# Small VectorE instructions of the tile tables and of the weight scales read one operand from PSUM

## Chip, core and metric

The kernel runs on one core of one Trainium2 chip. The metric is device time in microseconds (us) for one execution, in runs of the same program. Names of engines in the profile: PE is TensorE (PEld its weight loads), DVE is VectorE, ACT is ScalarE, POOL is GpSimd, SP is the queue that issues most DMAs.

## What is computed

Two layers in sequence: a causal convolution whose seven weights per head and position come from a softmax, then a mixture of experts that sends each of 28,672 tokens to one of eight experts.

```python
def _attn_ref(x, weight_gen):              # x (8, 3584, 192), weight_gen (8, 3584, 8, 7)
    w = np.exp(weight_gen - np.max(weight_gen, axis=-1, keepdims=True))
    w = w / (np.sum(w, axis=-1, keepdims=True) + 1e-09)
    x_pad = np.concatenate([np.zeros((B, pad, D)), x], axis=1)
    x_unf = x_pad[:, idx, :].reshape(B, S, K, H, group)
    return np.einsum('bshk,bskhg->bshg', w, x_unf).reshape(B, S, D)

def _moe_ref(x, w_gate, w_output_gate, w1, w2):   # x (28672, 192), w1 (8, 192, 1024), w2 (8, 1024, 192)
    logits = x @ w_gate
    e_idx = np.argmax(logits, axis=1)
    gate_w = probs[np.arange(N), e_idx]           # probs: softmax of logits
    eom = 1.0 / (1.0 + np.exp(-(x @ w_output_gate)))
    for e in range(E):
        mask = e_idx == e
        ye = np.maximum(x[mask] @ w1[e], 0.0) @ w2[e]
        out[mask] = gate_w[mask, None] * eom[mask, e, None] * ye
```

## The kernel before

**Units.** The tokens pass in 32 units of 896 (128 partitions by 7 rows). For each unit the seven weights per head go through a softmax (`softmax_steps`, line 506), seven products of shifted inputs with a weight are formed and added up (`tap_steps`, `acc_steps`). GpSimd forms five of the seven products in the later units (`gap` in the profile), VectorE the other two (into `ps` and `vt`), and VectorE adds all of them into an accumulator in PSUM; in the first seven units TensorE does the adding (`vap` and `gap` with `cf`). The sum is scaled and split into two float16 parts (`rt`), the expert is found (`sum_steps`), the position of each token in its expert's list is worked out (`place_steps`), and GpSimd scatters the rows into a sorted buffer in DRAM (`srtd`, seven indirect DMAs per unit).

**Tables of tiles.** After each unit a round decides how many tiles of T sorted tokens (512 in most rounds, 128, 256 or 384 in a few) have become full. `round_table` (line 844) works it out for R tiles at most on one partition of VectorE: `f_nE` is the number of tokens that each expert has and that no tile has taken (from `bs` and `done`); `gg` compares it with what the r-th tile needs; `cs` is a running count over experts; `f_cx` is that count, clipped to R, at each expert's end; `zt` is the row where an expert's next tile would begin, less T times the tiles counted before it; `ge` compares the count with r; `done` moves on; `dz` is the difference of neighbouring `zt`; two sums over `ge` then give the expert and the first row of each tile (`ti`), which SP reads into registers to load the tile. Small values that VectorE uses lie in `few`, columns 2320 to 2512 of the one PSUM tile `ps`, under names that begin with `f_`.

**Weights.** Eight experts' weights are loaded in float32, scaled by powers of two and split into two float16 parts (`split_steps`, line 431), in the first stage of the kernel. `scales` (line 375) takes the exponent of a sum of squares (`ex`) and makes of it the scale and its inverse; it works on two columns for weights (`wss` to `wsc` and `winv`), on one column for units (`ssq` to `sx` and `isx`) and for the gate.

**Tiles.** For each tile SP loads the sorted rows transposed (`xT`) and the expert's weights (`wa`, `wb`). TensorE makes the first product (`ps<-xT,wa`), ScalarE applies Relu into the float16 part `hh`, VectorE takes the rest of the value into `hl`, and TensorE makes the second product from `hh` and `hl`. ScalarE scales the result (`ys`), GpSimd sends it to its tokens by indirect DMA (`out_dram`).

**Order.** Instructions are written in the order that a planner in the kernel works out (`Order`, `Paced`): every step of a chain has a time that the planner estimates from sizes, and the chain that can go on first is written next. Each engine then runs its own instructions in that order, waiting on semaphores for the others. All instructions that pass through the planner have line L151 in the profile, so groups are told apart by their tiles. On VectorE the steps of a table, which yield to the planner one by one, stand between products, additions and `hl` steps of the same engine.

Of the kernel before, what the change touches and what calls it, by code (L numbers as in the profile page):

```python
# [11 lines left out]
F32 = mybir.dt.float32  # L12
I32 = mybir.dt.int32
AF = mybir.ActivationFunctionType
ALU = mybir.AluOpType
AX = mybir.AxisListType.X

P = 128
W = 194
WW = 3585  # L20
RMAX = 24
# [189 lines left out]
def kernel(ctx: ExitStack, tc: tile.TileContext, x, wg, wgate, wogate, w1, w2, cst, out):  # L211
    nc = tc.nc
    od = Order()
    V = Paced(od, nc.vector, vector_cost)
# [14 lines left out]
    CAP = N + 128  # L229
    DUMMY = NE * CAP  # L230
    plan = plan_rounds(NU, EVERY, P * JS)

    cp = ctx.enter_context(tc.tile_pool(name="cp", bufs=1))
# [5 lines left out]
    sp = ctx.enter_context(tc.tile_pool(name="sp", bufs=3))  # L239
# [24 lines left out]
    ps = pp.tile([P, 4096], F32, name="ps")  # L264
    turn = ps[:, 1536:1920].bitcast(F16)

    few = ps[:, 2320:2512]
# [1 line left out]
    f_m, f_se, f_ru = few[:, 56:63], few[:, 56:63], few[:, 64:72]  # L269
    f_e8 = few[:, 72:80]  # L270
    f_mx = few[:, 80:136]
    f_nE, f_one, f_cx, f_dz, f_tf = few[0:1, 136:144], few[0:1, 144:145], few[0:1, 145:154], few[0:1, 154:163], few[0:1, 163:179].rearrange("p (a b) -> p a b", a=2)
    mx_free, few_free = [0.0], [0.0]
    wa_free, wb_free, h_free, hu_free, y_free = [(0.0, "wa")] * WA, [(0.0, "wb")] * WB, [0.0] * HB, [], []
    st_free, tap_free = [0.0] * STG, {k + "a": [(0.0, k + "a")] * 2 + [(0.0, k + "t")] for k in "vg"}
# [54 lines left out]
    rr = cf[0:1, o : o + RMAX * 9].rearrange("p (a b) -> p a b", b=9)  # L330
# [5 lines left out]
    nc.vector.tensor_copy(f_e8, cf[:, o : o + 8])  # L336
    e8b = f_e8.unsqueeze(1).broadcast_to([P, JS, 8])

    done = cp.tile([1, 8], F32, name="done")
    base = cp.tile([P, NE], F32, tag="base", bufs=4, name="base0")  # L340
    for e in range(NE):
        nc.vector.memset(base[:, e : e + 1], float(e * CAP - 1))
        nc.vector.memset(done[:, e : e + 1], float(e * CAP))
    nc.vector.memset(f_cx[:, 0:1], 0.0)
    nc.vector.memset(f_one, 1.0)
    zt = cp.tile([1, 10], F32, name="zt")
    nc.vector.memset(zt[:, 0:1], 0.0)
    nc.vector.memset(zt[:, 9:10], float(DUMMY))
    pad = cp.tile([P, W], I32, name="pad")
    nc.gpsimd.memset(pad, 0)  # L350
    nc.gpsimd.memset(pad[:, 193:194], 65535)
# [23 lines left out]
    def scales(ssq, sc, inv, name, free=None):  # L375

        n = ssq.shape[1]
        ex = sp.tile([P, n], I32, tag=f"ex{n}", name=f"ex_{name}")
        V.tensor_scalar(ex, ssq.bitcast(I32), 1, MASK, op0=ALU.arith_shift_right, op1=ALU.bitwise_and)
        if free is not None:  # L380
            free.append(od.cur.t)
        yield V
        V.tensor_scalar(sc.bitcast(I32), ex, -1.0, float(197 << 23), op0=ALU.mult, op1=ALU.add)
        V.tensor_scalar(inv.bitcast(I32), ex, float(57 << 23), None, op0=ALU.add)
# [4 lines left out]
    def gate_steps():  # L389
        g32 = cp.tile([P, 4, 8], F32, name="g32")  # L390

        for i, w in enumerate((wgate, wogate)):
            SP.dma_start(out=g32[:, i, :], in_=w[0:128, :])
            SP.dma_start(out=g32[0:64, 2 + i, :], in_=w[128:192, :])
            SP.dma_start(out=g32[64:128, 2 + i, :], in_=w[128:192, :])
        yield S
        gsq = cp.tile([P, 32], F32, name="gsq")
        gss = cp.tile([P, 1], F32, name="gss")
        S.activation(gsq, g32.rearrange("p a b -> p (a b)"), AF.Square, accum_out=gss)
        yield T_  # L400
        pg = ps[:, 2304:2320]
        T_.matmul(pg[:, 0:1], lhsT=ones32, rhs=gss, start=True, stop=True)
        yield V
        sg = cp.tile([P, 1], F32, name="sg")
        isg = cp.tile([P, 1], F32, name="isg")
        yield from scales(pg[:, 0:1], sg, isg, "g")

        gm = cp.tile([P, 2, 32], F16, name="gm")
        g2 = g32.rearrange("p (c a) b -> p c (a b)", a=2)
        yield S  # L410
        S.activation(gm[:, :, 0:16], g2, AF.Copy, scale=sg)
        yield V
        V.scalar_tensor_tensor(out=gm[:, :, 16:32], in0=g2, scalar=sg, in1=gm[:, :, 0:16], op0=ALU.mult, op1=ALU.subtract)
        gates.update(isg=isg, mm=(gm[:, 0, :], gm[:, 1, :], gm[:, 0, :]))
# [16 lines left out]
    def split_steps(e, st1, st2):  # L431
# [9 lines left out]
        sc = sp.tile([P, 2], F32, tag="wsc", name=f"wsc{e}")  # L441
        inv = sp.tile([P, 2], F32, tag="winv", name=f"winv{e}")
        yield from scales(pg[:, 0:2], sc, inv, f"w{e}", tr_free)
        s1, s2 = sc[:, 0:1], sc[:, 1:2]
        yield from take(wa_free, S)
# [199 lines left out]
    def sum_steps(u):  # L645
# [11 lines left out]
        sx = sp.tile([P, 1], F32, tag="sx", name=f"sx{u}")  # L657
        isx = d["isx"] = sp.tile([P, 1], F32, tag="isx", name=f"isx{u}")
        yield from scales(ssq, sx, isx, f"x{u}")
        yield S  # L660
        S.activation(rt[:, :, 0:D], a3, AF.Copy, scale=sx)
# [182 lines left out]
    def round_table(r, T, R, tail, bs):  # L844

        nm = f"{r}"
        V.tensor_tensor(out=f_nE, in0=bs[0:1, :], in1=done, op=ALU.subtract)
        yield V

        gg = sp.tile([1, 8 * RMAX], F32, tag="gg", bufs=1, name=f"gg{nm}")[:, 0 : 8 * R]  # L850
        V.tensor_tensor(out=gg.rearrange("p (e r) -> p e r", r=R), in0=f_nE.unsqueeze(2).broadcast_to([1, 8, R]), in1=need["tail" if tail else T][:, 0:R].unsqueeze(1).broadcast_to([1, 8, R]), op=ALU.is_ge)
        yield V
        cs = sp.tile([1, 8 * RMAX], F32, tag="cs", bufs=1, name=f"cs{nm}")[:, 0 : 8 * R]
        V.tensor_tensor_scan(out=cs, data0=f_one.broadcast_to([1, 8 * R]), data1=gg, initial=0.0, op0=ALU.mult, op1=ALU.add)
        yield V
        V.tensor_scalar(f_cx[:, 1:9], cs.rearrange("p (e r) -> p e r", r=R)[:, :, R - 1], float(R), None, op0=ALU.min)
        yield V
        V.scalar_tensor_tensor(out=zt[:, 1:9], in0=f_cx[:, 0:8], scalar=-float(T), in1=done, op0=ALU.mult, op1=ALU.add)
        ge = sp.tile([1, RMAX, 9], F32, tag="ge", bufs=1, name=f"ge{nm}")[:, 0:R, :]
        V.tensor_tensor(out=ge, in0=f_cx.unsqueeze(1).broadcast_to([1, R, 9]), in1=rr[:, 0:R, :], op=ALU.is_le)  # L860
        yield V
        V.scalar_tensor_tensor(out=done, in0=f_cx[:, 1:9], scalar=float(T), in1=zt[:, 1:9], op0=ALU.mult, op1=ALU.add)
        dz = f_dz
        V.tensor_tensor(out=dz, in0=zt[:, 1:10], in1=zt[:, 0:9], op=ALU.subtract)
        tf = f_tf if R <= 8 else sp.tile([1, 2, RMAX], F32, tag="tf", name=f"tf{nm}")
        V.tensor_reduce(out=tf[:, 0, 0:R], in_=ge[:, :, 1:8], axis=AX, op=ALU.add)
        yield V
        V.tensor_tensor(out=ge, in0=ge, in1=dz.unsqueeze(1).broadcast_to([1, R, 9]), op=ALU.mult)
        yield V
        V.tensor_reduce(out=tf[:, 1, 0:R], in_=ge, axis=AX, op=ALU.add)  # L870
        yield V
        V.scalar_tensor_tensor(out=tf[:, 1, 0:R], in0=rr[:, 0:R, 0], scalar=float(T), in1=tf[:, 1, 0:R], op0=ALU.mult, op1=ALU.add)
        yield V
        if R > 8:
            ti = sp.tile([1, 2, RMAX], I32, tag="til", bufs=1, name=f"ti{nm}")
        else:
            ti = sp.tile([1, 2, 8], I32, tag="ti", bufs=NU // 2 + 6, name=f"ti{nm}")

        V.tensor_scalar(ti[:, :, 0:R], tf[:, :, 0:R], float(DUMMY), None, op0=ALU.min)
        yield V  # L880
        return ti
# [3 lines left out]
    def round_steps(u):  # L885

        found, bs = [], U[u]["base"]
        yield V, lambda: state["rounds"] == u
        for k, (T, R) in enumerate(plan[u]):
            tail = u == NU - 1 and k == len(plan[u]) - 1  # L890
            pads = None
            if tail:
                pads = sp.tile([1, NE], I32, tag="bi", name="bi")
                bf = sp.tile([1, NE], F32, tag="bf", name="bf")
                V.tensor_scalar(bf, bs[0:1, :], 1.0, None, op0=ALU.add)
                yield V
                V.tensor_copy(pads, bf)
            ti = yield from round_table(f"{u}_{k}", T, R, tail, bs)
            for i in range(R):
                found.append((T, ti, i, pads if i == 0 else None))  # L900
        state["rounds"] += 1
        yield SP, has(u, "sent")
        queue.extend((*f, max(od.cur.t, U[u]["sent_t"])) for f in found)
        if u == NU - 1:
            state["all"] = True
            queue[:] = mixed(queue)
            front.close()
            late.append(ctx.enter_context(tc.tile_pool(name="late", bufs=LATE_W, side="right", reuse_waits="tile")))
            wa_free.extend([(od.cur.t, "late")] * LATE_W)
            wb_free.extend([(od.cur.t, "late")] * LATE_W)  # L910
# [285 lines left out]
```

## Time and profile before

| what | value |
|---|---|
| median of three runs | 1300.61 us (1295.26 to 1304.66) |
| profiled execution | 1304.16 us |
| its span, first to last instruction | 1302.4 us |
| TensorE matmuls busy | 1147.5 us, 88% of the span, 9958 instructions |
| VectorE busy | 1021.3 us, 78%, 2103 |
| GpSimd busy | 895.0 us, 69%, 776 |
| ScalarE busy | 601.8 us, 46%, 1305 |
| mean granted TensorE clock | 0.968 |
| chain that ended last | PE 38%, DVE 27%, POOL 10%, issue 10%, DMA 9%, ACT 3% |

How to read the rows: `out<-in` are the program's names with buffer numbers left out, then shapes (partitions x elements and type), then the count. A row of a group gives busy us in total and the mean duration of one in ns, and after the bar the idle time of the engine just before these instructions with what ended it. A row of the timeline gives start and duration in us, and in brackets the idle time before it with its releaser. A row of waits gives us in total, how many times, and the longest. An instruction counts as busy from its start to its end, also where something holds it up after its start.

### The profile page before, as it was taken

The page shows a single profiled execution, that of the slowest core. Times are in us where ns is not written, and L with a number is a line of the kernel's source. Part 1 is how long each engine was busy: PE and PEld are TensorE (multiplying, and loading weights), DVE is VectorE, ACT ScalarE, POOL GpSimd, SP SyncE. Part 2 cuts the span into 40 slices and gives each one's busy share as a digit, 9 for nine tenths or more (in the row PEclk, how much of TensorE's full clock was granted, in tenths as well). Part 3 has the DMA queues.
Part 4 walks back from the last instruction along what each step waited for, and adds up shares of the span by engine and source line. Part 5 has one row for each costly group of instructions (what it writes and reads, how often), then busy time and mean ns, then how long its engine had stood idle before and what let it go on. Part 6 is the DMA issues. An engine that isn't in the chain of part 4 may idle for free.

```text
span 1302.4 us, 28065 instructions
## 1 busy us (share of the span) xinstructions
PE 1147.5 (88%) x9958; PEld 834.1 (64%) x9958; DVE 1021.3 (78%) x2103; ACT 601.8 (46%) x1305; POOL 895.0 (69%) x776
## 2 busy tenths in 40 slices
PE   5886947898697988999997999989899999979998
PEld 2443426676464766676665766666566779878998
DVE  8898866999999999999999999999998633323332
ACT  3674642454353544554454554445454443434443
POOL 7689666667878887888898878998878534322222
PEclk9999878999898999999998999999999999999999
DMA  7777579889777977978797897768867899999994
GB/s 237 228 242 225 175 239 246 226 227 249 201 215 214 241 203 202 272 213 216 205 258 163 262 249 236 202 203 237 211 165 201 220 295 305 320 283 327 308 341 137
DMA packets 293853, 306.18 MB, mean 235 GB/s; under 512 B 232278, under 2 KB 253639, under 8 KB 283344
## 3 DMA queue, kind: packets, MB, share of 16 engines
q1 hardware_dynamic: 271728, 259.78, 70.7%
q0 software_dynamic: 21840, 44.30, 10.6%
q8 instruction: 78, 1.28, 0.4%
q14 instruction: 63, 0.52, 0.1%
q10 hardware_dynamic: 144, 0.31, 0.1%
HBM read 196.42 MB, written 62.01 MB: 198 GB/s over the span
## 4 chain that ended last, share of the span: by engine, by line
PE 38%; DVE 27%; POOL 10%; issue 10%; DMA 9%; ACT 3%; SPq 2%; POOLq 0%; DVEq 0%; ACTq 0%
PE ps L151 38%; DVE ps L151 13%; POOL gap L151 6%; DVE hl L151 4%; POOL srtd L151 3%; SPq L125 2%; DMA w<-in_wg_dram 2%; DVE vap L151 2%; DVE rt L151 2%; DMA wa<-wd 2%; POOL out_dram L151 2%; DMA srtd<-rt,posi 1%; ACT rt L151 1%; DVE w L151 1%; DVE vt L151 1%
## 5 line engine op out<-in xcount | busy, mean ns | idle before, releaser
L151 PE MATMUL ps<-xT,wa 128*128 128x512 f16 (+3 forms) x3240 | 561.1, 324 | 67.0 <-DVE hl L151 30.7
L151 PE MATMUL ps<-wb,hh 128*128 128x192 f16 x3696 | 479.6, 247 | 17.3 <-ACT ys L151 10.5
L151 DVE SCALAR_TENSOR_TENSOR hl<-ps,hh 128x512 f16<-128x512 f32 (+1 forms) x476 | 310.9, 666 | 191.4 <-ACT hh L151 188.3
L151 PE MATMUL ps<-wb,hl 128*128 128x192 f16 x1848 | 456.4, 247 | 0.0
L151 PEld LDWEIGHTS <-wa 128*128 128x128 f16 x3240 | 279.7, 99 | 259.3 <-issue 51.2
L151 POOL TENSOR_TENSOR gap<-x,w 128x960 f32<-128x960 f32 (+5 forms) x268 | 372.4, 1414 | 36.0 <-DVE w L151 13.3
L151 ACT ACTIVATE hh<-ps 128x512 f16<-128x512 f32 (+1 forms) x476 | 274.9, 583 | 229.3 <-PE ps L151 228.5
L151 PEld LDWEIGHTS <-hh 128*128 128x128 f16 x3696 | 337.7, 98 | 65.8 <-issue 25.1
L151 POOL DMA_INDIRECT out_dram<-ys,meta x216 | 214.3, 992 | 235.2 <-ACT ys L151 161.9
L151 POOL DMA_INDIRECT srtd<-rt,posi x224 | 230.0, 1027 | 90.7 <-issue 57.9
L151 ACT ACTIVATE ys<-ps,sc 128x192 f32<-128x192 f32 x231 | 97.1, 421 | 236.1 <-PE ps L151 153.5
L151 DVE TENSOR_TENSOR ps<-ps,gap 128x1344 f32<-128x1344 f32 x125 | 194.1, 1553 | 7.3 <-POOL gap L151 6.4
L151 PEld LDWEIGHTS <-hl 128*128 128x128 f16 x1848 | 181.7, 98 | 0.2
L151 POOL TENSOR_TENSOR gap<-halo,w 128x1152 f32<-128x1152 f32 (+4 forms) x38 | 62.4, 1642 | 18.9 <-issue 13.1
L151 PE MATMUL ps<-gap,cf 128*128 128x512 f32 x168 | 71.9, 566 | 2.7 <-POOL gap L151 2.7
L151 PE MATMUL ps<-vap,cf 128*128 128x512 f32 (+1 forms) x126 | 57.0, 596 | 13.1 <-DVE vap L151 13.1
L151 DVE SCALAR_TENSOR_TENSOR rt<-ps,sx,rt 128x448 f16<-128x448 f32 x64 | 57.6, 907 | 8.4 <-ACT rt L151 4.9
L151 PE MATMUL ps<-gm,gt 128*128 128x32 f16 x672 | 28.1, 177 | 41.0 <-ACT ys L151 12.3
L151 PEld LDWEIGHTS <-gt 128*128 128x128 f16 x672 | 25.2, 96 | 50.9 <-issue 35.7
L151 ACT ACTIVATE rt<-ps 128x1344 bf16<-128x1344 f32 x32 | 41.3, 1291 | 25.4 <-DVE ps L151 20.7
L151 PEld LDWEIGHTS ps<-gap,cf 128*128 128x128 f32 x168 | 31.3, 196 | 32.6 <-issue 26.8
L151 PEld LDWEIGHTS ps<-vap,cf 128*128 128x128 f32 x126 | 24.8, 208 | 36.8 <-issue 23.1
(115 smaller groups left out, 868.7 us busy)
## 6 DMA issues: line engine op xcount, KB each, us to landing
wa<-wd SPq DMA_DIRECT2D x81, 1024.0 KB
wb<-wd SPq DMA_DIRECT2D x81, 768.5 KB
x<-in_x_dram SPq DMA_DIRECT2D x32, 672.0 KB
w<-in_wg_dram SPq DMA_DIRECT2D x32, 196.0 KB
wd<-wpb SPq DMA_DIRECT2D x8, 768.5 KB
st<-in_w_dram SPq DMA_DIRECT2D x8, 768.0 KB
st<-in_w_dram SPq DMA_DIRECT2D x8, 512.0 KB
wd<-wpa SPq DMA_DIRECT2D x8, 512.0 KB
```

The costliest lines, as they stand in the source:

```text
L125: r = f(*args, **kwargs)
L151: r = f(*args, **kwargs)
```

## The change

In `round_table` the operands change places. `done` moves from SBUF to PSUM (`f_done`), `f_cx` from PSUM to SBUF (`cx`). `zt`, which was one row in SBUF, becomes two: eight values and a constant in SBUF (`zt`), and a copy shifted by one in PSUM (`f_zt`), so it is computed twice. The row numbers `rr` are copied to PSUM once at the start (`f_rr`), because `cx`, their partner, lies in SBUF now. In `scales` the exponent of the weights (two columns) goes to two columns of PSUM (`f_ex`); with one column it stays in SBUF. Every VectorE instruction of a table that takes two tensors then has one in SBUF and one in PSUM, where R is 8 at most. The step from `cs` to `cx`, which takes one tensor, has its source and now also its destination in SBUF.

```diff
@@ names in PSUM
-    f_nE, f_one, f_cx, f_dz, f_tf = few[0:1, 136:144], few[0:1, 144:145], few[0:1, 145:154], few[0:1, 154:163], few[0:1, 163:179].rearrange("p (a b) -> p a b", a=2)
+    f_nE, f_one, f_done, f_dz, f_tf = few[0:1, 136:144], few[0:1, 144:145], few[0:1, 145:153], few[0:1, 154:163], few[0:1, 163:179].rearrange("p (a b) -> p a b", a=2)
+    f_ex = ps[:, 2536:2538].bitcast(I32)
+    f_zt, f_rr = few[0:1, 179:189], ps[0:1, 2512 : 2512 + RMAX]
@@ start
-    done = cp.tile([1, 8], F32, name="done")
...
-        nc.vector.memset(done[:, e : e + 1], float(e * CAP))
-    nc.vector.memset(f_cx[:, 0:1], 0.0)
+        nc.vector.memset(f_done[:, e : e + 1], float(e * CAP))
+
+    cx = cp.tile([1, 9], F32, name="cx")
+    nc.vector.memset(cx[:, 0:1], 0.0)
     nc.vector.memset(f_one, 1.0)
-    zt = cp.tile([1, 10], F32, name="zt")
-    nc.vector.memset(zt[:, 0:1], 0.0)
-    nc.vector.memset(zt[:, 9:10], float(DUMMY))
+    zt = cp.tile([1, 9], F32, name="zt")
+    nc.vector.memset(f_zt[:, 0:1], 0.0)
+    nc.vector.memset(zt[:, 8:9], float(DUMMY))
+    nc.vector.tensor_copy(f_rr, rr[:, :, 0])
@@ scales
-        ex = sp.tile([P, n], I32, tag=f"ex{n}", name=f"ex_{name}")
+        ex = f_ex if n == 2 else sp.tile([P, n], I32, tag=f"ex{n}", name=f"ex_{name}")
@@ round_table
-        V.tensor_tensor(out=f_nE, in0=bs[0:1, :], in1=done, op=ALU.subtract)
+        V.tensor_tensor(out=f_nE, in0=bs[0:1, :], in1=f_done, op=ALU.subtract)
...
-        V.tensor_scalar(f_cx[:, 1:9], cs.rearrange("p (e r) -> p e r", r=R)[:, :, R - 1], float(R), None, op0=ALU.min)
-        yield V
-        V.scalar_tensor_tensor(out=zt[:, 1:9], in0=f_cx[:, 0:8], scalar=-float(T), in1=done, op0=ALU.mult, op1=ALU.add)
+        V.tensor_scalar(cx[:, 1:9], cs.rearrange("p (e r) -> p e r", r=R)[:, :, R - 1], float(R), None, op0=ALU.min)
+        yield V
+        for z in (zt[:, 0:8], f_zt[:, 1:9]):
+            V.scalar_tensor_tensor(out=z, in0=cx[:, 0:8], scalar=-float(T), in1=f_done, op0=ALU.mult, op1=ALU.add)
         ge = sp.tile([1, RMAX, 9], F32, tag="ge", bufs=1, name=f"ge{nm}")[:, 0:R, :]
-        V.tensor_tensor(out=ge, in0=f_cx.unsqueeze(1).broadcast_to([1, R, 9]), in1=rr[:, 0:R, :], op=ALU.is_le)
-        yield V
-        V.scalar_tensor_tensor(out=done, in0=f_cx[:, 1:9], scalar=float(T), in1=zt[:, 1:9], op0=ALU.mult, op1=ALU.add)
+        V.tensor_tensor(out=ge, in0=cx.unsqueeze(1).broadcast_to([1, R, 9]), in1=f_rr[:, 0:R].unsqueeze(2).broadcast_to([1, R, 9]), op=ALU.is_le)
+        yield V
+        V.scalar_tensor_tensor(out=f_done, in0=cx[:, 1:9], scalar=float(T), in1=f_zt[:, 1:9], op0=ALU.mult, op1=ALU.add)
         dz = f_dz
-        V.tensor_tensor(out=dz, in0=zt[:, 1:10], in1=zt[:, 0:9], op=ALU.subtract)
+        V.tensor_tensor(out=dz, in0=zt, in1=f_zt[:, 0:9], op=ALU.subtract)
```

## The prediction

> **What bounds the kernel now.** I read the page first, then one view of windows, cut at the two places where the page's slices change character (TensorE steadies after the seventh slice, VectorE falls off after the thirty-first), then what the engines waited for, then the small VectorE groups one by one.
>
> ```profile
> span 1302.4 us, 28065 instructions
> ```
>
> ```profile
> 0.00:228.00 228.00, 165.17 (x787) 93.53 (x788) 183.32 (x350) 112.91 (x203) 162.56 (x123) 0.90 0.74 228
> 228.00:1021.00 793.00, 713.25 (x6159) 507.57 (x6157) 741.11 (x1559) 379.22 (x870) 645.36 (x564) 0.98 0.81 218
> 1021.00:1302.40 281.40, 269.10 (x3015) 233.04 (x3014) 96.86 (x195) 109.70 (x234) 87.04 (x89) 0.99 0.90 288
> ```
>
> The columns of the second fence are the stretch, its length, busy time of TensorE matmuls, weight loads, VectorE, ScalarE and GpSimd with instruction counts, TensorE's granted clock, DMA share and GB/s. There are three stages. Up to 228 us weights are split and the first units pass. From 228 to 1021 us VectorE is busy 741 of 793 us (93%), GpSimd 645 (81%), TensorE 713 (90%). After 1021 us TensorE alone is full, on work that is the same however early it starts. So the end moves if the middle stage gets shorter, and the most that could come out of it is TensorE's idle time there, 793 - 713 = 80 us.
>
> VectorE's busy time in the middle is not all work:
>
> ```profile
> L151 DVE TENSOR_TENSOR ps<-base,done x31: 152/165/5236, 132.2 to 1038.8; 1x8 f32<-1x8 f32 x31
> L151 DVE SCALAR_TENSOR_TENSOR zt<-ps,done x31: 142/148/157, 134.0 to 1039.8; 1x8 f32<-1x8 f32 x31
> ```
>
> ```profile
> L151 DVE TENSOR_TENSOR ps<-zt x31: 163/166/3914, 134.5 to 1042.0; 1x9 f32<-1x9 f32 x31
> ```
>
> The three durations are minimum, median and maximum in ns. All three groups stand in the table of tiles and work on eight or nine numbers of one partition. The one with an operand in PSUM (`zt<-ps,done`) never takes longer than 157 ns; the two with both operands in SBUF take up to 5236 and 3914. Where the long ones end can be laid against GpSimd, two of VectorE first, then two of GpSimd:
>
> ```profile
> 316.39 2.12 DVE L151 TENSOR_TENSOR ps<-zt 1x9 f32<-1x9 f32 x1
> ...
> 846.68 3.91 DVE L151 TENSOR_TENSOR ps<-zt 1x9 f32<-1x9 f32 x1
> ```
>
> ```profile
> 315.77 2.71 POOL L151 TENSOR_TENSOR gap<-x,w 128x576 f32<-128x576 f32 x2
> ...
> 845.20 5.36 POOL L151 TENSOR_TENSOR gap<-x,w 128x960 f32<-128x960 f32 x4
> ```
>
> 316.39 + 2.12 = 318.51 against 315.77 + 2.71 = 318.48; 846.68 + 3.91 = 850.59 against 845.20 + 5.36 = 850.56. The small instruction is let go when GpSimd's run of products ends. That is waiting, counted as busy.
>
> **The change part by part.** First what the waiting amounts to. Group, busy us, mean ns, then idle time:
>
> ```profile
> L151 DVE TENSOR_TENSOR ps<-base,done 1x8 f32<-1x8 f32 x31 | 32.4, 1045 | 0.9
> ...
> L151 DVE TENSOR_TENSOR ps<-zt 1x9 f32<-1x9 f32 x31 | 24.5, 789 | 1.1
> ...
> L151 DVE TENSOR_SCALAR wsc<-ex_w 128x2 int32<-128x2 int32 x8 | 6.7, 835 | 0.1
> ...
> L151 DVE TENSOR_SCALAR winv<-ex_w 128x2 int32<-128x2 int32 x8 | 1.3, 157 | 0.0
> ```
>
> The subtraction at the head of the table: 32.4 - 31 x 0.165 = 27.3 us. The difference `dz`: 24.5 - 31 x 0.166 = 19.4 us. Both lose their second SBUF operand (`done`, one of the two `zt`), so 46.6 us of VectorE time should go. The scales of the weights: 6.7 - 8 x 0.157 = 5.4 us.
>
> How much of VectorE's waiting reaches the end? Directly behind three of the stalls TensorE waited for `hl`, the evacuation that VectorE had queued behind the stalled instruction:
>
> ```profile
> 464.08 3.16 DVE L151 TENSOR_TENSOR ps<-base,done 1x8 f32<-1x8 f32 x1
> ```
>
> ```profile
> 320.69 0.97 PE L151 MATMUL ps<-xT,wa 128*128 128x384 f16 x5 [1.89 <-DVE hl L151]
> ...
> 470.47 1.24 PE L151 MATMUL ps<-xT,wa 128*128 128x512 f16 x5 [1.64 <-DVE hl L151]
> ...
> 852.56 1.24 PE L151 MATMUL ps<-xT,wa 128*128 128x512 f16 x5 [1.89 <-DVE hl L151]
> ```
>
> Stalls of 2.12, 3.16 and 3.91 us, less 0.16 each, are 8.7 us; TensorE's waits behind them are 5.42 us, a share of 0.62. The chain that ended last gives an upper end: twelve of these stalls lie on it as pieces of their own, 32.9 us together, or 0.71 of 46.6; the first and the last of the twelve:
>
> ```profile
> 305.95 3.15 DVE ps L151
> ...
> 995.28 1.44 DVE ps L151
> ```
>
> The lowest of the three pairs, 1.89 behind 3.75, is 0.50. I take 0.62.
>
> Now what the change puts in. `cx`, the clipped running count, moves from PSUM to SBUF. Its step reads `cs` in SBUF and now writes SBUF too: one source, eight elements, nothing in PSUM. The nearest rows are the scale steps, which also have one source and lie wholly in SBUF:
>
> ```profile
> L151 DVE TENSOR_SCALAR sx<-ex_x x32: 127/146/155, 38.5 to 1005.4; 128x1 int32<-128x1 int32 x32
> ```
>
> ```profile
> L151 DVE TENSOR_SCALAR wsc<-ex_w x8: 160/854/1845, 32.0 to 159.4; 128x2 int32<-128x2 int32 x8
> ```
>
> With one element per partition, 32 of them never exceeded 155 ns; with two, the median is 854 ns. So a one-source instruction of several elements waits as the two-source ones do, and the new `cx` step has eight. It is the second wait that the change may add: behind it VectorE has `hl` queued as before, and TensorE waits for `hl`. GpSimd's products end early enough that not all 31 tables meet one:
>
> ```profile
> L151 POOL TENSOR_TENSOR gap<-x,w x268: 515/1534/3192, 12.0 to 1000.0; 128x576 f32<-128x576 f32 x29, 128x960 f32<-128x960 f32 x27, 128x768 f32<-128x768 f32 x27, 128x384 f32<-128x384 f32 x22
> ```
>
> ```profile
> 1026.88 0.16 DVE L151 TENSOR_TENSOR ps<-base,done 1x8 f32<-1x8 f32 x1
> ...
> 1038.75 0.15 DVE L151 TENSOR_TENSOR ps<-base,done 1x8 f32<-1x8 f32 x1
> ```
>
> Four tables start after 1000.0 us (these two are the first and the last). For the other 27, at the scale step's mean excess of 835 - 157 = 678 ns, the `cx` step takes 18.4 us; the ends are 0 (it does not wait) and 27 x 0.88 = 23.8 us (the excess of `ps<-base,done`). I take 18.4, since the scale step is the same kind of instruction. What keeps doubt is that `cs` is read with a stride of R elements, which no row shows for such an instruction. Left of the 46.6 us are 28.2, and 28.2 x 0.62 = 17.5 us of the time.
>
> The Trainium skill has a rule that speaks against this part. Its page VectorE: DVE Perf Modes, section What auto-detection actually checks, says that an instruction with one source goes into a mode with two SBUF ports when source and destination are in SBUF and their outermost counts are even, and it names no condition on the step; SBUF — State Buffer, section Who interferes with whom, says that an instruction in such a mode and GpSimd shut each other out. The trace agrees in the two rows of `sx` and `wsc`; no row here shows it for a strided source. By that rule the sum is the one above; without it, the second rival's.
>
> The twin of `zt` is one more instruction per table, written to PSUM beside the SBUF one, so that the later steps have one operand in each. Its price is `zt<-ps,done`'s, 31 x 0.148 = 4.6 us, of which 0.62 is 2.9 us; between nothing, where VectorE would have waited anyway, and 4.6. The planner that works out the order of the instructions is charged for it as well, so its order can shift; it is not told of the stalls, so nothing else moves it. I take 0, with the largest single wait of TensorE for weights on either side:
>
> ```profile
> PE ps L151 <- DVE hl L151: 30.7, 21, 4.8
> PE ps L151 <- DMA wa<-wd: 29.5, 8, 6.5
> ```
>
> That is 6.5 us up or down. `wsc` stands in the first stage, where VectorE is busy 183 of 228 us and where a two-operand split of the weights follows it and meets the same products; half of the 5.4 us, 2.7, is my value, 0 and 5.4 the ends. Its intermediate goes to columns beside `few`, in a stretch of PSUM that TensorE also writes in this stage; what that may cost in waits between the two has no row, and I let it lie within the same 5.4 us, from the other side. The copy of the row numbers to PSUM at the start and the swap of `rr` for it exchange one PSUM operand for another and cost nothing that counts: 0.17 us once, beside loads.
>
> The sum: -17.5 - 2.7 + 2.9 = -17.3 us. The profiled execution took 1304.16 us (its span 1302.4 and 1.8 around it) and lies 3.6 above the median of three, 1300.61. So 1304.16 - 17.3 = 1286.9 for that execution, and 1283 against the median.
>
> **The rivals.** *The new `cx` step does not wait.* Then all of 46.6 us count: 46.6 x 0.62 = 28.9, sum -28.7, 1272 us. For it: no row shows a strided source waiting. Against it: `wsc`.
>
> *Something else is late next.* VectorE saves its 28.2 us, but arrives earlier at sums that need GpSimd's products, and the product that held the stall is often the one it needs; GpSimd at 81% has less room than its share suggests, and TensorE's waits for weights (29.5 us) stay. If a quarter gets through in place of 0.62, 7.0 us, the sum is -6.8 and the time 1294. Against it: TensorE's largest wait by name is `hl`, 30.7 us in 21 times.
>
> *Slower: the `cx` step waits for all that GpSimd does.* GpSimd's queue holds row scatters between the products; the two-operand steps are let go at those. If the `cx` step is not, it waits to the end of an unbroken stretch of GpSimd work. Its place is each of the 27 tables; at 3.0 us each (the stall at 464.08) it costs 81 us, against 46.6 removed: +34.4 x 0.62 = +21.3, sum +21.5, 1322 us. It turns into a loss from a mean wait of 46.6 / 27 = 1.7 us. For it: GpSimd's 81%. Against it:
>
> ```profile
> 37.70 0.62 DVE L151 TENSOR_SCALAR wsc<-ex_w 128x2 int32<-128x2 int32 x1
> ```
>
> ```profile
> 31.15 10.26 POOL L151 TENSOR_TENSOR gap<-x,w 128x960 f32<-128x960 f32 x6 [0.69 <-PE ps L151]
> ```
>
> Here it was let go at 38.32, in the midst of six products that lasted to 41.41. The same section of the Trainium skill's SBUF — State Buffer limits the two-operand clash to GpSimd instructions that read SBUF, and has no such limit for the two-port modes; the trace shows no scatter holding a scale step.
>
> That the change does not do what it says, an operand in PSUM that leaves the wait in place, is excluded by `zt<-ps,done`: 31 times in the same tables, 157 ns at most.
>
> **How the numbers follow.** Chances: forecast 0.42, no wait at `cx` 0.25, something else late 0.21, slower 0.12. The range: at the low end no wait at `cx`, with the chain's share and all of the scales, 33.1 + 5.4 - 2.9 = 35.6 us less, 1265; at the high end the third case with the planner's 6.5 us and a little of the slower one, 1304. Left out are about 0.10 above and 0.08 below. One per cent, about what a measurement of this kernel can tell from no change, is 13 us: faster means below 1287.6, slower above 1313.6. The forecast with its own bounds (share 0.50 to 0.71, planner's shift) lies below 1287.6 in about 0.7 of its cases, 0.30; the second case whole, 0.25; of the third 0.03: faster 0.58. Slower is 0.10, most of the last case. Same is the remaining 0.32.
>
> **What would show it.** In the changed kernel the head of the table and `dz` should have maxima near 0.17 us, and their groups some 5 us each. The step from `cs` to `cx` decides between the first two cases: a mean near 0.8 us with ends at ends of GpSimd's products, or 0.15. TensorE's waits for `hl` should fall from 30.7 to some 15 us, and the middle stage should end some 17 us sooner with the last stage as long as before. I am wrong if those waits fall and the end of the middle stage stays (third case), if the `cx` group passes 47 us (slower), or if TensorE's waits turn up at other names because the order moved.

## The result and the profile after

The changed kernel takes 1301.65 us (median of 20 runs, 1297.25 to 1312.17), the kernel before 1302.89 us in 20 runs beside it; the ratio is 1.000 with a 95% interval of 0.9978 to 1.0022. The profiled execution took 1304.84 us. No difference, then, where 17 us were forecast; the time lies near the upper end of the range.

VectorE's small instructions did what was expected of them. Groups of the changed kernel by form (busy us, mean ns, idle before):

```profile
L151 DVE TENSOR_SCALAR cx<-cs 1x8 f32<-1x8 f32 x31 | 24.5, 790 | 0.1
...
L151 DVE TENSOR_TENSOR ps<-zt,ps 1x9 f32<-1x9 f32 x31 | 4.9, 159 | 1.1
L151 DVE TENSOR_TENSOR ps<-base,ps 1x8 f32<-1x8 f32 x31 | 4.9, 157 | 0.9
...
L151 DVE SCALAR_TENSOR_TENSOR zt<-cx,ps 1x8 f32<-1x8 f32 x31 | 4.5, 146 | 0.4 <-PE ps L151 0.2
```

The head of the table and `dz`, 32.4 and 24.5 us before, are at 4.9 us each. The `cx` step, which lies in SBUF wholly, has become the new waiter: 24.5 us, of which 31 x 0.15 = 4.7 are work. Its longest wait, on VectorE's timeline (start, duration, then the instruction) and on GpSimd's:

```profile
523.73 0.17 DVE L151 TENSOR_TENSOR_SCAN cs<-ps,gg 1x16 f32<-1x16 f32 x1
...
525.16 3.83 DVE L151 TENSOR_SCALAR cx<-cs 1x8 f32<-1x8 f32 x1
```

```profile
523.60 5.36 POOL L151 TENSOR_TENSOR gap<-x,w 128x576 f32<-128x576 f32 x4
529.13 1.01 POOL L151 DMA_INDIRECT out_dram<-ys,meta  x1 [0.17 <-issue]
```

525.16 + 3.83 = 528.99 against 523.60 + 5.36 = 528.96: it waits out a run of products and is let go ahead of the next scatter. Of the 31 `cx` steps 13 took over 0.4 us; each of them ended within 0.04 us of the end of a product, ten with a scatter next and three with another product. This `cs` has 16 elements, so R is 2 and the step reads every second one. VectorE is busy 23 us less in the middle stage (717.76 us against 741.11), but the stage is no shorter. The same windows as in the prediction:

```profile
228.00:1021.00 793.00, 720.82 (x6205) 512.31 (x6203) 717.76 (x1584) 380.46 (x873) 647.08 (x566) 0.98 0.82 221
1021.00:1302.40 281.40, 263.08 (x2947) 227.80 (x2946) 94.74 (x195) 106.81 (x228) 84.98 (x87) 0.99 0.89 279
```

TensorE got 46 more matmuls done up to 1021 us (6205 against 6159) and had less left, yet ended at the same time. What it waited for (us in total, times, longest):

```profile
PE ps L151 <- DMA wa<-wd: 45.3, 13, 10.6
...
PE ps L151 <- DVE hl L151: 12.3, 10, 3.0
PE ps L151 <- DMA gt<-rt: 11.2, 10, 2.4
```

Waits for `hl` fell from 30.7 to 12.3 us, as forecast. Waits for tile weights rose from 29.5 to 45.3 us, those for a unit's transposed rows (`gt`) from 1.2 to 11.2. And the order is another one. TensorE's matmul for the ranks of the last unit, which the last table needs, in the kernel before and in the changed one:

```profile
1025.78 0.17 PE L151 MATMUL ps<-p,upper 128*128 128x8 f16 x1
```

```profile
1027.45 0.18 PE L151 MATMUL ps<-p,upper 128*128 128x8 f16 x1
```

It starts 1.7 us later, and in the order it stands behind 5882 matmuls of tiles where it stood behind 5814. The planner had written 68 more of them ahead of it.

So there were two theories. **A**: the planner, charged for the twin of `zt` (its second copy, in PSUM), wrote an order that costs what the operands won. **B**: weight loads are the next bound in any order, and operands can win nothing.

### The profile page after: what moved, and what is told of

Its sections match the earlier page's. It is cut to its first block, busy times and chain, and to the rows that moved or that the text cites. A ratio compares the mean times of both kernels' runs of the same rounds, so it can differ in the third digit from the quotient of the medians.

```text
span 1303.1 us, 28117 instructions
## 1 busy us (share of the span) xinstructions
PE 1150.5 (88%) x9958; PEld 835.3 (64%) x9958; DVE 996.2 (76%) x2135; ACT 600.4 (46%) x1305; POOL 895.5 (69%) x776
## 4 chain that ended last, share of the span: by engine, by line
PE 36%; DVE 16%; DMA 7%; POOL 5%; issue 5%; SPq 3%; ACT 2%; POOLq 0%; DVEq 0%; ACTq 0%
PE ps L151 36%; DVE ps L151 7%; DMA wa<-wd 4%; DVE hl L151 4%; POOL gap L151 3%; SPq L125 3%; DMA gt<-rt 2%; POOL out_dram L151 1%; POOL srtd L151 1%; DVE vt L151 1%; DVE rt L151 1%; DVE cx L151 1%; ACT rt L151 1%; DMA srtd<-rt,posi 1%; ACT hh L151 1%
## 5 line engine op out<-in xcount | busy, mean ns | idle before, releaser
L151 PE MATMUL ps<-xT,wa 128*128 128x512 f16 (+3 forms) x3240 | 563.8, 326 | 58.1 <-DMA wa<-wd 45.3
L151 PE MATMUL ps<-gm,gt 128*128 128x32 f16 x672 | 29.7, 178 | 48.4 <-DMA gt<-rt 11.2
```

The costliest lines, as they stand in the source:

```text
L151: r = f(*args, **kwargs)
```

## Experiments

Each kernel was timed in five rounds beside the kernel before on the same chip; ratios are to that. "Old order" means that every engine runs its instructions in the sequence of the kernel before, "new order" in that of the changed kernel. The runs came in four batches, each on a chip of its own: e1 to e4, e5 to e8, e9 to e12, e13 to e16.

**Operands and order apart.** e1 issues the twin past the planner, so the planner is not charged for it and writes the old order:

```diff
-        for z in (zt[:, 0:8], f_zt[:, 1:9]):
-            V.scalar_tensor_tensor(out=z, in0=cx[:, 0:8], ...)
+        for z, eng in ((zt[:, 0:8], V), (f_zt[:, 1:9], nc.vector)):
+            eng.scalar_tensor_tensor(out=z, in0=cx[:, 0:8], ...)
```

> The changed kernel, with the twin of zt issued past the planner, so that every engine's order is that of the kernel before and only operands (and one small instruction per table) differ. Theory A, the planner's charge for the twin shifted the order and the new order costs what the operands won: about 1285 us (46.6 us of stalls less the 19.8 us that now stand at cx, times 0.62, and a little for the twin), TensorE's waits for hl near 12 us, the ranks of the last unit some 10 us earlier than before, and waits for tile weights no more than before's 29.5 us. Theory B, weight loads are the next bound in whatever order: within 4 us of before (1302.9), with waits for tile weights near 45 us.

e2 is the opposite, the kernel before with the charge and without the instruction:

```diff
         V.scalar_tensor_tensor(out=zt[:, 1:9], in0=f_cx[:, 0:8], ...)
+        V.t = max(V.t, od.cur.t + V.before) + vector_cost("", (zt[:, 1:9],), {})
+        od.cur.t = max(od.cur.t, V.t + V.after)
```

> The kernel before with the planner charged for a twin that is not issued: operands of before, order of the changed kernel. Theory A: about 1318 us, slower than before by what the operands won (16 us). Theory B: the order is indifferent, within 4 us of before (1302.9).

e3 is the changed kernel with the `cx` step made a two-operand instruction, one of them a one in PSUM; e4 is e1 with the same edit.

```diff
-        V.tensor_scalar(cx[:, 1:9], cs...[:, :, R - 1], float(R), None, op0=ALU.min)
+        V.scalar_tensor_tensor(out=cx[:, 1:9], in0=cs...[:, :, R - 1], scalar=float(R), in1=f_one.broadcast_to([1, 8]), op0=ALU.min, op1=ALU.mult)
```

> The changed kernel in its own order, with the cx step given a second operand in PSUM (a one to multiply with), so that it no longer has everything in SBUF. The cx group should fall from 24.5 us to about 4.7 (0.15 each). If VectorE's remaining stalls still count at 0.62: 12 us less than the changed kernel, about 1290 us. Theory B: no change, 1298 to 1305 us.

> Both: order of before, cx step without its wait. Theory A with the price of 0.62 for each us of stall: about 1273 us (46.6 us of stalls gone, 28.9 us of time). Theory B: within 4 us of before (1302.9).

| operands | old order | new order |
|---|---|---|
| as before (all stalls) | 1 | e2: 1.0148 (1.0122 to 1.0174) |
| as changed (stall at `cx`) | e1: 0.9919 (0.9889 to 0.9948) | the change: 1.0000 (0.9978 to 1.0022) |
| no stalls at tables | e4: 0.9863 (0.9838 to 0.9889) | e3: 0.9907 (0.9876 to 0.9937) |

The kernel before took 1304.28 us beside e1 to e4. Theory B falls: the order alone, with not one operand changed, costs 1.48% or 19 us, and in the old order the change's operands win 0.81% or 11 us. Theory A holds in the main, though not in its sizes: e1 came out at 1294.5 us, not 1285, and kept 39.8 us of waits for weights where no more than 29.5 were expected; e2 took 1323.8 us, not 1318, e3 1293.4, not 1290, and e4 1287.3, not 1273. Operands and order do not simply add: the order costs 1.48% with the operands as before, 0.81% with those of the change and 0.44% without stalls, there with intervals that overlap. The order's mark can be seen at the ranks of the last unit, in e1 and in e2:

```profile
1013.46 0.17 PE L151 MATMUL ps<-p,upper 128*128 128x8 f16 x1
```

```profile
1043.74 0.17 PE L151 MATMUL ps<-p,upper 128*128 128x8 f16 x1
```

Against 1025.78 before, the operands bring it 12 us forward and the order puts it 18 us back.

Not all that the order costs is waiting. In the profiled executions TensorE's matmuls are busy 1157.5 us in e2 and 1147.5 us before, which is 10 of the 15 us between the two spans (1317.2 and 1302.4 us), and the granted clock is lower: 0.957 to 0.963 in the six runs of e2, 0.963 to 0.968 in the eleven of the kernel before beside them. Whether the order lowers the clock was not looked into. Between e1 and the changed kernel, which have the same operands, the profiled clocks are alike (0.966 and 0.965), and the difference is idle time of TensorE: 1292.0 - 1149.4 = 142.6 us against 1303.1 - 1150.5 = 152.6 us.

The wait of the `cx` step was worth 0.93% in the new order (0.9907 against 1.0000) and 0.56% in the old one. Its group in e3:

```profile
L151 DVE SCALAR_TENSOR_TENSOR cx<-cs,ps 1x8 f32<-1x8 f32 x31 | 4.6, 148 | 0.9 <-PE ps L151 0.7
```

From 790 to 148 ns. The edit turned the step into a two-operand instruction, but what counts is that something lies in PSUM: in the kernel before, the same one-operand step with its destination in PSUM took 153 ns:

```profile
L151 DVE TENSOR_SCALAR ps<-cs 1x8 f32<-1x8 f32 x31 | 4.7, 153 | 0.8 <-PE ps L151 0.4
```

With all 46.6 us of stalls gone, e4 won 1.37%, 18 us: 0.38 of each us, not 0.62 (the scales and the twin are in this, too).

**What takes the stalls' place.** In e4 TensorE waits at 704.55 us for weights, where the wait of the kernel before, in the same place of the order, is put down to VectorE (e4 first, then before):

```profile
704.55 1.89 PE L151 MATMUL ps<-xT,wa 128*128 128x512 f16 x4 [6.25 <-DMA wa<-wd]
```

```profile
713.14 2.32 PE L151 MATMUL ps<-xT,wa 128*128 128x512 f16 x5 [6.40 <-DVE ps L151]
```

A wait of 6.40 us became one of 6.25. The weights had been as late before: SP issued them there 6.5 us ahead of the matmuls, in e4 6.4 us ahead. This is the row before:

```profile
706.63 0.40 SPq L125 DMA_DIRECT2D wa<-wd  x1
```

In the trace of the kernel before, the last of the weights landed at 713.09 us and VectorE signalled at 713.11, so an earlier VectorE wins 0.02 us here. SP's queue in e4 tells why the weights are late:

```profile
695.83 0.43 SPq L125 DMA_DIRECT2D meta<-srtd  x1
696.40 1.58 SPq L125 DMA_TRANSPOSE xT<-srtd  x1
698.19 0.41 SPq L125 DMA_DIRECT2D wa<-wd  x1
```

```profile
SPq L125 <- DMA srtd<-rt,posi: 162.7, 45, 10.2
```

The weights (`wa`) are issued 2.4 us behind the rows (`meta`, `xT`), and rows wait for GpSimd's scatters to land: 2.8 us at this place, 162.7 us over the execution, the longest of SP's waits. Weights need nothing of the scatters, only the expert's number. So e5 is e4 with a tile's two weight loads ahead of its row loads, and e6 the kernel before with the same exchange. The planner is charged as it was, so the orders of the other engines stay.

```diff
     def tile_load(t, T, ti, i, writers, ka, kb):
...
+        nc.sync.dma_start(out=wa, in_=wd[bass.ds(e, 1), :, 0:2048]...)
+        nc.sync.dma_start(out=wb, in_=wd[bass.ds(e, 1), :, 2048:WW]...)
         loaded(SP.dma_start(out=meta[:, 0:Gn, :], ...), writers)
         loaded(SP.dma_start_transpose(out=xT[:, :, 0:T], ...), writers)
-        SP.dma_start(out=wa, ...)
-        SP.dma_start(out=wb, ...)
+        for o in (wa, wb):
+            SP.issued = max(SP.issued, od.now) + sync_issue("dma_start", (), {"out": o})
+            SP.moved = max(SP.moved, SP.issued + 0.65) + sync_cost("dma_start", (), {"out": o})
+            od.cur.t = max(od.cur.t, SP.moved + 1.0)
```

> The kernel without stalls in the old order (e4), with a tile's two weight loads issued ahead of its row loads on SP, all other engines' orders kept. Theory C, what is late after the stalls are gone is the weight load, because it stands in SP's queue behind row loads that wait for GpSimd's scatters: TensorE's waits for weights between 228 and 1010 us fall from 20.8 us to under 8, and the time by 8 to 13 us, to about 1277 us. Theory D, the weights are late because DMA engines are full: the waits only change their name (rows instead of weights), 1284 to 1291 us.

> The kernel before with the same exchange on SP, stalls kept. Theory C: at most the 11.3 us of waits for weights that it has between 228 and 1010 us, some 4 to 7 us of time, about 1298 us; then stalls removed are worth 20 us or more with weights first, against 17 without. Theory D: 1300 to 1308 us.

e5: 0.9795 (0.9762 to 0.9829), 1275.84 us. e6: 0.9990 (0.9965 to 1.0016), 1301.28 us; the kernel before took 1302.98 us beside them. With the stalls in place the exchange is worth nothing that can be measured; with them gone it is worth 0.7%, 9 us (the ratio of e5 against that of e4 from another chip). Stalls and late weights stand in each other's cover. Between e6 and e5 the stalls are worth 1.95%, 25 us, or 0.55 of each us. The time of e5 is that of theory C, in which weights queued behind rows are what holds TensorE; that of e6 lies in the range of theory D. And the waits did not vanish. TensorE's waits in e5 between 228 and 1010 us:

```profile
PE ps L151 <- DMA xT<-srtd: 18.6, 5, 7.1
PE ps L151 <- DVE hl L151: 7.9, 10, 1.8
```

Waits for weights are none, but 18.6 us for rows have come, nearly the 20.8 us for weights in e4, which is what theory D, that the wait only changes its name, said of the names. At the three places where e4 waits longest for weights in this stretch, 6.86, 6.59 and 6.25 us, e5 waits 5.26, 3.79 and 7.08 us for rows: shorter at two, and longer at the third, the place shown above. The gain was made early: the ranks of the tenth unit (numbered 9) come at 328.9 us in e4 and 318.5 in e5, those of the last at 1012.6 and 996.3. The traces overstate it, since e4's profiled execution, 1293.17 us, is the slowest of its six. So theory C has the time for it, and a full account of the 9 us by waits is missing.

**The order, once more.** e7 and e8 charge the planner of e4 for half a step and for two steps, which gives two further orders; the latency that the planner adds to a step is charged whole in e7 and twice in e8.

> e4's instructions, with the planner charged for half of a step (chain latency whole). Another order. If a different order is worth what chance gives it: anywhere from 1280 to 1305 us. If the charge as such does harm in proportion: between e4 (1287) and e3 (1293).

> e4's instructions, with the planner charged for two steps. If order is chance: anywhere from 1280 to 1305 us. If the charge does harm in proportion: about 1300 us, 6 us beyond e3.

e7: 0.9955 (0.9931 to 0.9979); e8: 0.9922 (0.9891 to 0.9952). With the same instructions, charges of none, half, one and two steps give 0.9863, 0.9955, 0.9907 and 0.9922. That is not in proportion to the charge: another order looks like another draw, and the four lie 0.9% apart. But all three charged orders are slower than the uncharged one, so a harm common to any charge is not excluded by four orders. By the planner's own numbers, the charge of the twin's time alone, 0.08 us, would leave the order as it was; what shifts it is the 0.13 us of latency that the planner adds for the step. That was worked out and not timed.

**Single terms.** These four ran on another chip, where the kernel before takes 1359.45 us; only ratios among them are used. e9 is e5 with `cx` wholly in SBUF again, e10 is e5 with the scales' exponent back in SBUF, e11 the kernel before with only the scales changed (the line of the change in `scales`), e12 is e3 with weights first.

> e5 (weights first, old order, no stalls) with the cx step as the change has it, all in SBUF. Its group should go from about 4.5 to 22 us again. If a stall counts at 0.62 where weights are not late: 11 us more than e5, about 1287 us. If at the 0.36 that e4 showed: 6 us, about 1282 us. If VectorE is no longer what TensorE waits for: 1276 us.

> e5 with the exponent of the weight scales back in SBUF: 5.4 us of stalls return in the first stage. By the prediction's half: 2.7 us more than e5, 1278.5 us. If the first stage has cover for all of it: 1276 us. If the whole counts: 1281 us.

> The kernel before with nothing changed but the exponent of the weight scales, which goes to PSUM; order unchanged. The prediction's half: 2.7 us less, 1300 us. With cover: 1303 us. A loss, by waits between TensorE and VectorE in the shared stretch of PSUM: above 1305 us.

> e3 (order of the change, no stalls) with weights first. If weights first is worth as much in this order as in the old one (11.5 us): about 1282 us, and the order still costs 6 us against e5. If the new order's cost was itself the late weights (it had longer waits for them): 1276 us, no difference to e5.

e9: 0.9830 (0.9787 to 0.9874), e10: 0.9761 (0.9719 to 0.9803), e11: 1.0015 (0.9986 to 1.0043), e12: 0.9750 (0.9709 to 0.9791). The scales win nothing alone (e11), though their own stalls are gone there:

```profile
L151 DVE TENSOR_SCALAR wsc<-ps 128x2 int32<-128x2 int32 x8 | 1.2, 153 | 0.1
```

Before, this group took 6.7 us. The wait at `cx` brings its group to 21.5 us in e9, 17 us more than without it. Since e5 was not timed on this chip, its price is read against e10 (which has the scales' stalls) and e12 (which has the new order): 0.7 and 0.8%, 9 to 11 us or some 0.6 of each us, with intervals that overlap a little. And e12 in the new order is no slower than e10 in the old one, where e3 had been slower than e4. The last batch put the orders side by side, on a chip where the kernel before takes 1303.61 us: e13 repeats e5, e14 repeats e12, e15 is e2 with weights first, e16 repeats e2.

> e5 again, as the reference on the same chip for the next two. Ratio to the kernel before 0.975 to 0.983.

> e12 again (order of the change, no stalls, weights first), beside e13 on one chip. Theory F, the new order costs time because it lets more of the weight loads come late: no difference to e13 (under 4 us). Theory G, the new order is worse by itself, whatever SP does: 6 us or more above e13, as e3 lay above e4.

> e2 (operands of before, order of the change, slower than before by 1.5%) with weights first. Theory F: the 1.5% goes, ratio 0.995 to 1.003, as e6 had in the old order. Theory G: ratio 1.010 to 1.018, since the old order gained nothing from weights first while the stalls stood.

> e2 again on the same chip as e15, as its reference: ratio 1.010 to 1.018 to the kernel before.

| weights first | old order | new order |
|---|---|---|
| no stalls | e13: 0.9798 (0.9770 to 0.9826) | e14: 0.9806 (0.9777 to 0.9834) |
| all stalls | e6: 0.9990 (0.9965 to 1.0016) | e15: 1.0054 (1.0032 to 1.0075) |
| all stalls, weights in their old place | 1 | e16: 1.0140 (1.0108 to 1.0172) |

Without stalls and with weights first the order costs nothing that can be measured. With stalls it costs 1.40%, of which weights first takes away 0.86 and leaves 0.54; against e6, the old order with weights first on another chip, 0.64 are left. e15 lies between the ranges of the two theories, nearer to F, so theory F holds for the larger part: with the stalls the new order loses time mostly where a tile's weights come late. The changed kernel's longest wait for weights shows such a place, on TensorE and on SP:

```profile
481.39 2.31 PE L151 MATMUL ps<-xT,wa 128*128 128x512 f16 x5 [10.56 <-DMA wa<-wd]
```

```profile
471.85 0.42 SPq L125 DMA_DIRECT2D meta<-srtd  x1
472.43 1.62 SPq L125 DMA_TRANSPOSE xT<-srtd  x1
474.24 0.43 SPq L125 DMA_DIRECT2D wa<-wd  x1
```

TensorE had nothing from 470.83 us on, SP had waited 2.5 us for scatters, issued rows at 471.85 and weights at 474.24, and the matmuls began at 481.39, 7.2 us behind the issue. What remains with stalls was not followed further; totals of waits by name do not explain it (waits for rows are 40.0 us in e15 and 45.5 in e14, which is the faster).

## Why the prediction was wrong

The step that failed is the planner's: "I take 0, with the largest single wait of TensorE for weights on either side", 6.5 us up or down. The new order measured +1.48% and +1.40%, 18 to 19 us, with the operands as before (e2, e16), and +0.81%, 11 us, with those of the change (e1 against the change): beyond the bound both times. It takes back all that the operands win, which is 11 us in the old order (e1) and 19 in the new one (e2 against the change), where 17.3 were forecast. The order itself was moved by the charge alone, as the prediction said: e2 and the changed kernel run the same sequence on every engine, but for the twin. What failed is its price. The bound came from one wait, but an order decides all of them: which tiles' matmuls stand before a unit's ranks, and when each tile's loads are asked for. The prediction's last condition for being wrong, waits that turn up at other names because the order moved, is what the trace shows: 12.3 us for `hl`, but 45.3 for weights and 11.2 for transposed rows.

The steps that held: stalls of 46.6 us at the head of the table and at `dz` went, to 157 and 159 ns each. The new wait at `cx`, set at 18.4 us from the scale step, measured 24.5 - 4.7 = 19.8 us. The doubt about a strided source is settled: the longest wait, at 525.16 us, is a strided one. The Trainium skill, VectorE: DVE Perf Modes, section What auto-detection actually checks, names no condition on the step for that mode, and the trace agrees by these 3.83 us. The rival in which `cx` does not wait falls with them (the prediction calls it the second rival at one place; it is the first). The `cx` step did not wait for all that GpSimd does, since ten of its 13 long waits ended ahead of a scatter: the slower rival falls too. In the kernel before, 18 of 23 stalls over 0.4 us ended at the end of a run of products and five between two products, so that "when GpSimd's run of products ends" holds for most of them.

The share of 0.62 was too simple, and a second term that was mis-sized. It came from three pairs whose own shares are 0.96, 0.55 and 0.50. The chain's share is also a little higher than was read: thirteen stalls lie on it as pieces of their own, not twelve, 34.0 us together or 0.73. TensorE's waits for `hl` did fall by it, 30.7 to 12.3 us in the changed kernel, but what got through to the time was 0.38 of each us in the old order (e4), 0.55 with weights first (e5 against e6), and 2.41% or 31 us of 46.6, 0.67, in the new order (e2 against e3). In the old order weights were late next, right behind the stall; this is the mechanism of the rival "something else is late next", and it took some 8 of the 25 us. That rival had named GpSimd's products as what would be late, and beside them the waits for weights that stay; it was the weights, behind row loads that wait for GpSimd's scatters.

The scales' 2.7 us were nothing that can be measured (e11, 1.0015, interval down to 0.9986, which leaves 2 us possible). The twin's 2.9 us were not measured alone.

The best version is e5: old order, no small stalls, weights ahead of rows, 0.9795 and again 0.9798 (e13), 26 us under the kernel before. The same in the new order (e14, 0.9806) is no slower by any measure here.

## What to carry to other kernels

An edit to an operand that passes through a planner is two edits: check whether every engine's sequence is still the same, and if not, issue the new instruction past the planner or time the order by itself, with the charge and without the instruction. Removing a wait is worth what the next-late operand at that place leaves; look for it in the queue that issues it, and put first in a queue what waits for nothing. In this kernel a one-operand VectorE step with more than one element and everything in SBUF waits for GpSimd's products as a two-operand one does; a dummy operand in PSUM frees it (790 ns became 148).

## What was not expected of the hardware

The same kernel took 1303 to 1304 us on three chips and 1359 us on a fourth, 4% more, with TensorE's waits for ScalarE's `ys` about twice as long there (22.1 us in e5, 43.2 in e10 between 228 and 1010 us). In these two profiled executions, which differ by the scales alone, TensorE's matmuls are busy 1142.9 and 1160.4 us, its idle time is 130.6 and 166.8 us, and the granted clock 0.967 and 0.957. The cause was not looked for; comparisons across chips would have been wrong by more than the change is worth.
